# Warm-up matmuls in the prologue and the plan's hand-over times, in an attention and SwiGLU kernel on one core

## The chip, the core and the metric

The kernel runs on one core of one Trainium2 chip. A core has engines that run their own instruction streams and meet only at semaphores: TensorE (PE in the profile; its weight loads are listed as PEld), VectorE (DVE), ScalarE (ACT), GpSimd (POOL) and SyncE (SP), which here issues most DMAs. Matmuls write into PSUM, which the kernel uses as eight banks of 128 x 512 fp32. The metric is the device time of one execution in microseconds. It was taken in 14 runs; the number compared is their median.

## What is computed

A layer norm without weights, then two branches from the normalised rows: multi-query attention with 32 heads of width 16 that share one K and one V, and a SwiGLU feed-forward. The output is the input plus the product of the two branches, the second passed through one more SiLU.

```
S, D, H, Dh, F = 2048, 512, 32, 16, 1792
xn = layernorm(x)
q  = (xn @ wq) split into H heads;  k = xn @ wk;  v = xn @ wv      # k, v: [S, Dh]
p  = softmax(q k^T / sqrt(Dh));     s = (p v, heads joined) @ wo
b  = (silu(xn @ w_gate) * (xn @ w_up)) @ w_down
out = x + s * silu(b)
```

The score matrix has 32 * 2048 * 2048 entries, and each needs an exponential. That is the bulk of the work for ScalarE and VectorE.

## The kernel before

**Tiling.** Rows come in four blocks of 512 (NSC). Heads come in four groups of eight (NQ); a block of rows with a group of heads is a "pair", and a pair has two "halves" of four heads. That makes 32 blocks `b` of 16 key tiles times 2 head pairs `x`, so 1024 score tiles of 128 x 1024. Each tile is two matmuls (L813) into one of three double banks, `ring[0..2]`, and has one of two ways out:

- ScalarE reads `ring[0]` or `ring[1]` and writes exp to a bf16 buffer `Pb` (L863).
- VectorE reads `ring[2]` and writes a scaled 16-bit integer to `Ub` (L890). When two tiles of a pair are there, three more operations split it by bit masks into `Eb` (L906) and `Wb` (L903) and multiply (L908), so that two accumulating matmuls with differently scaled V give an approximation of the exponential.

Both ways end in matmuls with V (L696) that accumulate in `o_ps`, with the softmax's denominator beside it. At the end of a block VectorE copies `o_ps` to `oa` (L709). After both halves of a pair, small DMAs on SyncE's queue gather the denominators into `dn` (L723) and pack the second half's values (L667), VectorE takes the reciprocal (L670), and further DMAs (L673, L679) spread it for a multiplication on GpSimd (L681).

**Fill.** The feed-forward, the Q projections of later pairs and the output projections use the bank `m_ps` in between (L466 for their matmuls, L607 and L624 for their tanh on ScalarE, L592, L609, L613, L626, L640 on VectorE).

**Prologue.** Statistics (L415, L416), normalisation (L425), transposes on TensorE (L430) into banks that ScalarE or VectorE copies to `xnT` (L436), then K, Q and V of row block 0 (L439, L447, L443, L555, L452); row blocks 1 to 3 follow while the first score tiles run.

**What sets the order.** While the program is built, a small list scheduler (`_Sched`, L182) plays the whole kernel through in its own time and writes down an order for every engine, which the emitted instructions then follow. `sd.free[engine]` is when an engine is free in that plan. Each operation has a planned duration, for example 0.904 for an exp, 1.135 for L890, 0.6 for most 512-wide VectorE operations and 0.215 for a 512-column matmul (MMF). `avail(d, eng)` gives when the result of `d` may be used on another engine: its planned end plus `LAT` of the engine that made it. The tiles' own semaphores keep the data right whatever the plan says; the plan only decides who stands behind whom.

`pe_pick` chooses TensorE's next work: a score tile for ScalarE as soon as a ring slot is planned free, other ready work if it fits before that (with `TOL` = 0.12 of slack), a score tile for VectorE (`dve_sc`) or a "junk" matmul whose result nobody reads (L1100). Ahead of all planned work `NWARM` matmuls of the same kind stand in TensorE's stream (L411). The plan of the kernel before starts TensorE at 0 and doesn't know of them.

`dve_tile` decides whether VectorE gets a tile: in the last block only if at least `D_LIM_END` tiles of it are left for ScalarE, in the blocks before it `D_LIM`.

## Time and profile before

| | |
|---|---|
| median of 14 runs | 800.91 us (796.01 to 813.11) |
| profiled execution | 802.83 us |
| its span, first to last instruction | 801.0 us |
| mean granted TensorE clock | 0.969 |
| first exp starts | 20.70 us |
| exps on ScalarE, score tiles on VectorE | 774, 250 |

The page of the profile gives totals over the whole span; a second view gives each engine's busy time for chosen stretches; a third, the timeline, lists instructions in order of time with their start, their duration and, in square brackets, how long the engine stood idle before one and what ended that. Successive exps overlap in it[...]: the mean record of L863 is 1171 ns, and yet in busy stretches one starts every 0.9 us or so. The granted clock is 1.00 where TensorE runs at full rate.

### The profile page before, as it was taken

Reading aid. Unit: us, or ns where it says so; the run is one execution under the profiler, and the core shown is the slowest. Engines: PE = TensorE matmul, PEld = TensorE weight load, DVE = VectorE, ACT = ScalarE, POOL = GpSimd, SP = SyncE. Lnnn points to the kernel's source line nnn. Section 1 sums busy time; section 2 is a strip of 40 time slices with the busy share of each in tenths; the row PEclk is TensorE's granted clock in tenths of the full one; section 3 lists DMA queues with packets and bytes.
Section 4 is the critical chain, followed back from the end, with each engine's and each line's share of the span. In section 5 each row is a group of like instructions: output and inputs, shape, how many; then the busy total and the mean of one; then the engine's idle time right before and its main releaser. Section 6 shows DMA issues by size and latency. Waiting matters only on the chain.

```text
span 801.0 us, 19338 instructions
## 1 busy us (share of the span) xinstructions
PE 738.1 (92%) x8005; PEld 222.5 (28%) x8009; DVE 748.1 (93%) x935; ACT 754.1 (94%) x856; POOL 52.1 (7%) x59
## 2 busy tenths in 40 slices
PE   8889899899989999999999999999999999999994
PEld 4332222222212222222222222222222222222221
DVE  4879999999969999999999999999999999999985
ACT  2799999999979999999999999999999999999991
POOL 1210000000002000000002010000000210000001
PEclk9899999999979999999999999999999999999957
DMA  9300000000000000000001000000000010000000
GB/s 330 106 1 2 22 2 23 1 4 21 1 23 21 10 20 2 23 2 23 3 7 31 15 22 2 23 2 7 18 1 14 31 29 2 9 15 2 23 1 30
DMA packets 19463, 18.49 MB, mean 23 GB/s; under 512 B 8552, under 2 KB 15464, under 8 KB 19368
## 3 DMA queue, kind: packets, MB, share of 16 engines
q1 hardware_dynamic: 17496, 16.37, 6.7%
q8 instruction: 64, 1.05, 0.6%
q10 hardware_dynamic: 1872, 0.82, 0.4%
q14 instruction: 31, 0.25, 0.1%
HBM read 12.62 MB, written 2.34 MB: 19 GB/s over the span
## 4 chain that ended last, share of the span: by engine, by line
PE 37%; ACT 26%; DVE 25%; issue 8%; SPq 1%; DMA 1%; POOL 0%; ACTq 0%; DVEq 0%; POOLq 0%
ACT Pb L863 22%; PE ring L813 14%; PE m_ps L466 12%; DVE Ub L890 9%; PE o_ps L696 7%; DVE Wb L908 4%; ACT th L607 3%; DVE Wb L903 3%; DVE Eb L906 2%; SPq L723 1%; ACT th L624 1%; DVE ab L609 1%; DVE hT L613 1%; DVE oa L709 1%; PE ring L1100 1%
## 5 line engine op out<-in xcount | busy, mean ns | idle before, releaser
L863 ACT ACTIVATE Pb<-ring 128x1024 bf16<-128x1024 f32 x774 | 734.0, 1171 | 14.4 <-PE ring L813 13.4
L813 PE MATMUL ring<-QB,KT 32*128 32x512 bf16 x2048 | 323.2, 389 | 35.9 <-ACT Pb L863 25.5
L890 DVE TENSOR_SCALAR Ub<-ring 128x1024 uint16<-128x1024 f32 x250 | 304.9, 1219 | 15.9 <-PE ring L813 8.5
L813 PEld LDWEIGHTS <-KT 32*128 32x128 bf16 x2048 | 103.7, 91 | 341.7 <-issue 336.1
L908 DVE TENSOR_TENSOR Wb<-Wb,Ub 128x2048 f16<-128x2048 f16 x125 | 153.9, 1231 | 0.0
L696 PE MATMUL o_ps<-Pb,VA 128*32 128x512 bf16 x1548 | 149.6, 395 | 0.9 <-POOL VA L461 0.5
L903 DVE TENSOR_SCALAR Wb<-Ub 128x2048 uint16<-128x2048 uint16 x125 | 88.4, 707 | 0.3 <-PE o_ps L696 0.3
L906 DVE TENSOR_SCALAR Eb<-Ub 128x2048 uint16<-128x2048 uint16 x125 | 86.4, 691 | 0.0
L466 PE MATMUL m_ps<-xnT,wu_sb 128*32 128x512 bf16 x896 | 72.2, 388 | 3.6 <-DVE ab L609 3.6
L466 PE MATMUL m_ps<-wd_sb,hT 128*32 128x512 bf16 x896 | 73.2, 384 | 1.3 <-DVE g_sb L626 1.2
L466 PE MATMUL m_ps<-xnT,wg_sb 128*32 128x512 bf16 x896 | 73.8, 388 | 0.4 <-DVE hT L613 0.2
L681 POOL TENSOR_TENSOR oT<-oa,rb 128x512 bf16<-128x512 f32 x15 | 22.2, 1483 | 614.7 <-DMA rb<-dscr 551.8
L696 PE MATMUL o_ps<-Eb,VD 128*32 128x512 f16 x500 | 51.1, 398 | 2.9 <-DVE Eb L906 2.0
L696 PE MATMUL o_ps<-Wb,VD 128*32 128x512 f16 x500 | 50.5, 393 | 2.8 <-DVE Wb L908 2.3
L696 PEld LDWEIGHTS <-VA 128*32 128x32 bf16 x1548 | 37.1, 94 | 51.5 <-issue 51.0
L696 PEld LDWEIGHTS <-VD 128*32 128x32 f16 x1000 | 31.1, 94 | 50.6 <-issue 48.1
L607 ACT ACTIVATE th<-m_ps 128x512 f32<-128x512 f32 x56 | 42.3, 755 | 0.0
L613 DVE TENSOR_TENSOR hT<-ab,m_ps 128x512 bf16<-128x512 f32 x56 | 38.1, 681 | 2.2 <-PE m_ps L466 1.9
L609 DVE SCALAR_TENSOR_TENSOR ab<-th,m_ps 128x512 f32<-128x512 f32 x56 | 38.0, 679 | 1.9 <-ACT th L607 1.5
L466 PEld LDWEIGHTS <-wu_sb 128*32 128x32 bf16 x896 | 18.0, 95 | 34.3 <-issue 31.6
L709 DVE COPY oa<-o_ps 128x512 f32<-128x512 f32 (+1 forms) x33 | 21.9, 667 | 3.0 <-PE o_ps L696 3.0
L466 PEld LDWEIGHTS <-wg_sb 128*32 128x32 bf16 x896 | 16.5, 94 | 26.3 <-issue 26.0
(94 smaller groups left out, 242.6 us busy)
## 6 DMA issues: line engine op xcount, KB each, us to landing
rb<-dscr SPq DMA_DIRECT2D x15, 256.0 KB
dn<-oa SPq DMA_DIRECT2D x120, 2.0 KB, 1.7
oa<-oa SPq DMA_DIRECT2D x60, 32.0 KB, 2.0
wg_sb<-in_B_w_gate_dram SPq DMA_DIRECT2D x1, 1792.0 KB, 11.5
wu_sb<-in_B_w_up_dram SPq DMA_DIRECT2D x1, 1792.0 KB
wd_sb<-in_B_w_down_dram SPq DMA_DIRECT2D x1, 1792.0 KB, 20.4
out_dram<-xn SPq DMA_DIRECT2D x14, 128.0 KB, 1.7
x_sb<-in_A_x_dram SPq DMA_DIRECT2D x3, 512.0 KB
```

Source lines behind the costliest of these rows:

```text
L466: return [nc.tensor.matmul(out=dst[GRP * j:GRP * j + GRP, :], lhsT=w[:, GRP * j:GRP * j + GRP], rhs=rhs, start=start, stop=stop, tile_posi ...
L607: t_ = OP("ACT", 0.477, [a], lambda: nc.scalar.activation(out=th[i][:], in_=m_ps[:], func=ACT.Tanh, scale=0.5), (0,), name="tanh")
L609: s_ = OP("DVE", 0.6, [t_, ab_rel[i]], lambda: nc.vector.scalar_tensor_tensor(out=ab[i][:], in0=th[i][:], scalar=1.0, in1=m_ps[:], op0=ALU ...
L613: h = OP("DVE", 0.6, [b], lambda: nc.vector.tensor_tensor(out=hT[:, f, :], in0=ab[i][:], in1=m_ps[:], op=ALU.mult), (1,), name="hmul")
L696: r.append(nc.tensor.matmul(out=o_ps[GRP * g:GRP * g + GRP, :], lhsT=lhs, rhs=rhs, start=(n == 0), stop=(n == pv_total[(b, g)] - 1), tile_ ...
L709: oev[b] = sd.new(_Op("DVE", 0.6, [], lambda: [nc.vector.tensor_copy(out=oat[:, a:z], in_=o_ps[:, a:z]) for a, z in cuts], (0.2,), name="o ...
L813: return lambda: [nc.tensor.matmul(out=ring[sl][:, u * 512:(u + 1) * 512], lhsT=KT[half][GRP * g:GRP * g + GRP, t * P:(t + 1) * P], rhs=QB ...
L863: lambda: nc.scalar.activation(out=Pb[pi][:], in_=ring[i][:], func=ACT.Exp, scale=escale, bias=ebias),
L890: lambda: nc.vector.tensor_scalar(out=Ub[ui][:, x * 1024:(x + 1) * 1024], in0=ring[2][:], scalar1=ubias, scalar2=UINF, op0=ALU.add, op1=AL ...
L903: o1 = OP("DVE", 0.6, [pa, pa0, w_rel[u - NE] if u >= NE else None], lambda: nc.vector.tensor_scalar(out=Wb[ei][:], in0=Ub[ui][:], scalar1 ...
L906: o2 = OP("DVE", 0.6, [pa, pa0, e_rel[u - NE] if u >= NE else None], lambda: nc.vector.tensor_scalar(out=Eb[ei][:], in0=Ub[ui][:], scalar1 ...
L908: o3 = OP("DVE", 1.135, [o1, o2], lambda: nc.vector.tensor_tensor(out=Wb[ei][:].bitcast(FP16), in0=Wb[ei][:].bitcast(FP16), in1=Ub[ui][:]. ...
```

## The change

Six edits:

1. `NWARM` falls from 18 to 13, and the plan starts TensorE at 6.8 instead of 0. Junk matmuls may now be placed in any planned gap of over 0.3 as long as no VectorE pair has been started (before: as long as no feed-forward job had been), up to 200 instead of 60.
2. `LAT`, the planned time from the end of a ScalarE result to its use elsewhere, grows from 0.166 to 0.22; for VectorE from 0.13 to 0.25.
3. `D_LIM_END` grows from 6 to 8.
4. In `place_sc` a score tile of row block 0 depends on the half of K that it reads, not always on the second.
5. In `pe_do` a VectorE score tile that is put right behind a ScalarE one isn't planned before its K and Q.
6. At the end the build asserts that no operation is emitted ahead of one that it depends on.

```diff
-NWARM, NJUNK = 18, 60
-D_START, D_LIM, D_LIM_END = 26, 12, 6
+NWARM, NJUNK = 13, 200
+D_START, D_LIM, D_LIM_END = 26, 12, 8
...
-    LAT = {"PE": 0.205, "ACT": 0.166, "DVE": 0.13, "POOL": 0.16, "DMA": 0.0, "EXT": 0.0}
+    LAT = {"PE": 0.205, "ACT": 0.22, "DVE": 0.25, "POOL": 0.16, "DMA": 0.0, "EXT": 0.0}
...
     sd = _Sched()
+    sd.free["PE"] = 6.8
...
         ks = k_ready[t // 4][b % 2]
-        sc = _Op("PE", dur, [slot[sl]] + ks[-1:] + q_ready[b // 2], sc_emit(sl, b, t, x), (0,), "r", "sc")
+        ks = ks[t % 4 // 2:t % 4 // 2 + 1] if len(ks) > 1 else ks
+        sc = _Op("PE", dur, [slot[sl]] + ks + q_ready[b // 2], sc_emit(sl, b, t, x), (0,), "r", "sc")
...
-        junk = job["f"] == 0 and cur["junk"] < NJUNK and all(
+        junk = cur["np"] == 0 and cur["pair"] is None and cur["junk"] < NJUNK and all(
             w.start is None or v.start is not None and v.end + 0.13 <= F for w, v, bk in held if bk == "2b")
...
-            at = max(sd.free["PE"], sd.avail(slot[2], "PE"))
+            at = max(sd.free["PE"], sd.avail(slot[2], "PE"), tile_ready(*dt))
...
-    for o in order:
+    place = {id(o): i for i, o in enumerate(order)}
+    for i, o in enumerate(order):
+        assert all(d.eng == "EXT" or place[id(d)] < i for d in o.deps), [(o.name, o.start, o.seq)] + [(d.name, d.start, d.end, d.seq) for d in o.deps]
```

Counted in the two built programs, the change removes 5 matmuls of L411 and 28 of L1100, turns 4 VectorE tiles into exps (778 and 246), and leaves the number of every other kind of instruction as it follows from that. The order changes on TensorE, VectorE and ScalarE nearly everywhere.

## The prediction

> **What bounds the kernel now.** I read the page first, then the windows cut at the places where ScalarE stalls, then the timeline of the first 32 us, of the stall near 225 us and of the end. "Exp" below is one ScalarE activation of L863, a tile of 128x1024 scores; a "DVE tile" is one of the same size taken by VectorE at L890.

> From the page, the shares of busy time and the costliest groups:

> ```profile
> PE 738.1 (92%) x8005; PEld 222.5 (28%) x8009; DVE 748.1 (93%) x935; ACT 754.1 (94%) x856; POOL 52.1 (7%) x59
> ...
> L863 ACT ACTIVATE Pb<-ring 128x1024 bf16<-128x1024 f32 x774 | 734.0, 1171 | 14.4 <-PE ring L813 13.4
> L813 PE MATMUL ring<-QB,KT 32*128 32x512 bf16 x2048 | 323.2, 389 | 35.9 <-ACT Pb L863 25.5
> ```

> Three engines are nearly full, so the average says little. The windows say where they are not (stretch, length, then busy time of PE, weight load, VectorE, ScalarE, GpSimd, then the granted TensorE clock):

> ```profile
> 20.70:32.20 11.50, 9.74 (x85) 4.19 (x85) 8.78 (x23) 7.86 (x8) 2.94 (x5) 0.70 0.51 162
> 225.00:246.00 21.00, 18.96 (x156) 3.64 (x155) 15.30 (x19) 14.64 (x17) 2.51 (x2) 0.67 0.08 21
> 400.00:600.00 200.00, 188.71 (x2138) 56.25 (x2138) 195.46 (x231) 200.00 (x229) 12.70 (x8) 1.00 0.05 13
> 760.00:783.60 23.60, 22.85 (x140) 5.14 (x140) 20.82 (x30) 21.65 (x23) 0.00 (x0) 0.52 0.00 1
> 783.60:801.00 17.40, 6.50 (x85) 2.43 (x77) 8.47 (x23) 0.74 (x2) 2.75 (x2) 0.79 0.11 35
> ```

> From 400 to 600 us ScalarE never rests: there it is the bound. It starves only before its first exp, and in three stretches where the clock is low (0.70, 0.67, 0.52). Price of a saturated exp: from 246 to 760 us the groups list 533 exps and 52 tanhs; one tanh takes 0.48 from its start to the next start (439.07 to 439.55 in the timeline), so an exp takes (514 - 52*0.48)/533 = 0.917 us. So the span is: first exp at 20.70; 774*0.917 + 72*0.48 = 709.8 + 34.6 = 744.4 of saturated work; the last exp ends at 783.6, so 783.6 - 20.7 - 744.4 = 18.5 us lost in between; then 17.4 us of tail. Of the 18.5 I put 5.5 before 48 us (24 exps in 27.5 us), 6.3 at 225 to 246 (16 exps and a tanh in 21 us need 15.2), 3.4 at 760 to 783.6 (22 exps need 20.2), the rest scattered.

> Why the first exp is late, in the timeline:

> ```profile
> 1.41 6.64 PE L411 MATMUL ring<-QB,ident_bf 128*128 128x512 bf16 x18 [1.41 <-POOL ident_bf masks.py:199]
> ...
> 6.75 0.72 DVE L425 TENSOR_SCALAR xn<-x_sb,mv,rstd 128x512 bf16<-128x512 bf16 x2
> ...
> 7.88 6.85 PE L1100 MATMUL ring<-x_sb,ident_bf 128*128 128x512 bf16 x31
> ...
> 14.79 0.61 PE L430 MATMUL ring<-ident_bf,xn 128*128 128x128 bf16 x8
> ...
> 20.70 3.77 ACT L863 ACTIVATE Pb<-ring 128x1024 bf16<-128x1024 f32 x4 [0.48 <-PE ring L813]
> ```

> The normalised rows xn are ready from 7.1 us, but their transposes stand behind 18 + 32 dummy matmuls in TensorE's order and start at 14.79. The plan counted TensorE free from 0 and did not know of the 18. And the stall at 225 us:

> ```profile
> 219.93 0.69 DVE L709 COPY oa<-o_ps 128x512 f32<-128x512 f32 x1
> ...
> 225.75 0.35 DVE L670 RECIPROCAL rc<-dn 128x32 f32<-128x32 f32 x1 [2.47 <-DMA oa<-oa]
> ...
> 227.23 0.39 PE L813 MATMUL ring<-QB,KT 32*128 32x512 bf16 x2 [1.70 <-DVE Ub L890]
> ```

> VectorE stood 2.47 us at a reciprocal whose DMAs had not landed, TensorE 1.70 us behind it, and the clock then fell to 0.50 for 230 to 240 us.

> [...] the weight loads of L411 are 0.42 us apart until 6.50 us, closer from 6.80; windows of 2 and 5 us put the later spells at 0.50 at 23.7 to 30.6 (6.8 us) and 228.5 to 242.2. [...] Here an exp lasts 1.171 us while its successor starts 0.917 later, and a TensorE score that waits starts 0.05 after that end: 1.22 from exp start to release. [...] on the SyncE queue here 1.7 (dn) and 2.0 (oa).

> **The change, part by part** (the order is that of the built program, in which no time stands).

> 1. Warm-up and TensorE's start in the plan (NWARM 13, free at 6.8, the new gap rule). Ahead of the first transpose stand 13 + 1 dummies instead of 18 + 32. 13 at 0.427 from 1.41 end at 6.96, one more at 7.39; xn is there at 7.1 to 7.5. So the transposes start near 7.5, 7.3 us earlier. What follows (copy, K, Q, second half) has the same order and 4 + 4 dummies in its gaps as before. What could hold it: wq landed 4.9 us after its issue at 1.30, so 6.2, and its first matmul would come at 9.7; wv (1.82 + 7.0 = 8.8) at 13.4; the second pair of xn ends at 10.05, needed at 10.2. None binds. First exp: 20.70 - 7.2 = 13.5. FFN weights: wg 15.5 and wd 26.7, first FFN matmul moves from 51.5 to near 42: no wait. TensorE must be warm by then; the trace had it warm at 6.7, within the 13. [...]

> 2. The first 32 tiles. VectorE's order now has the last statistics of row block 1 before the K copies of block 0, and TensorE does that block's transposes two rows together. In the trace this chain (17.99 to K at 30.91) made ScalarE starve 2.90 us before 32.21. Its TensorE part ran cold. I take 2 of the 5.5 us back; ends: 0 and 4.

> 3. ACT 0.166 to 0.22, DVE 0.13 to 0.25. The plan's exp is 0.904, so it now frees a slot 1.124 after the start, against 1.22 measured and 1.07 before: nearer. For a VectorE op of 0.6 it has 0.85 against 0.68 + 0.05 measured: now too careful. TensorE's 25.5 us of waits for exps should shrink, but ScalarE at 100% hides them. Saturated exps have a floor: many are 0.90 apart. Gain at most (0.917 - 0.904)*778 = 10 us, loss taken as equal; value 0. What moves besides: on VectorE between the last o_ps copy and the reciprocal. Before, the shortest distance is 2.33 us of work (the stall at 225), the next 3.47 and 3.53; the reciprocals that waited least (0.16 and 0.31) started 3.62 and 3.84 after the copy's end. After, that one place has 3.47, but three have 2.87 to 2.93. Each waits about 0.7[...] unless a DMA is late, as dn was by 1.7 in 2 of 15 pairs. Behind the reciprocal stand all VectorE tiles, and behind them TensorE's scores. Instead of 6.3 I take 3; ends 0 and 3*6.3.

> 4. D_LIM_END 8 and the new latencies together: 778 exps and 246 DVE tiles instead of 774 and 250: +4*0.917 = +3.7 us of ScalarE; VectorE loses 9 us of work, hidden, as ScalarE is the bound. In return the end: the last exp ended at 783.6, but VectorE's last product only fed TensorE at 787.09, the o_ps copies at 787.53, the transposes of L938 at 788.01, and the end came 13.0 later. Now the last accumulation comes from an exp, with 24 wo matmuls (1.3 us) behind: transposes at 0.1 + 0.2 + 1.3 = 1.6 after the last exp, tail 14.6 instead of 17.4: -2.8. FFN matmuls now fill TensorE until 9 tiles are left instead of 33, so the cold stretch from 760 loses its cause: 1 instead of 3.4.

> 5. The pairing of K halves, the due time of a merged VectorE score, the assertion: order alone, no instruction; nothing.

> Sum: 13.5 + (778*0.917 + 34.6 = 748.0) + lost (3.5 + 3 + 1 + scattered 3 = 10.5) + 14.6 = 786.6, against the span of 801.0: -14.4. The profiled execution took 802.83, 1.92 above the median of 800.91; so the median would be 786.5.

> **Rivals.**
> - Only the start gains (0.20): later losses remain 18.5, since cold spells move rather than go. 13.5 + 748.0 + 18.5 + 14.6 = 794.6 span, median 794.5. [...] Against: order at 225 and at the end did change.
> - It does not do what it says: 13 dummies do not warm TensorE, which stays at half rate through the prologue (0.12). +3 to the first exp, +2 for block 1: 791.5. For it: the dummies stop 0.7 us after the release in the trace. Against: activity from 1.41 is unbroken.
> - Slower (0.10): reciprocals issued before their DMAs land, at the places with 2.87 to 3.47 us, five in all; each full cold spell costs 6.3. 783.5 + n*6.3: three give 802.4, four 808.7, five 815. It decides from about three. For it: one 2.47 us wait did this at 225. [...]

> **How the numbers follow.** The sum (0.58) gives 787; its own range 780 to 793 from the ends of steps 2 to 4. To 0.8 I go down to 779 and up to 797, which takes in the first two rivals. A measurement here tells 0.3% (2.4 us) from no change. Faster 0.90; same 0.04 (three spells); slower 0.06.

> **What would show it.** Right: first transpose near 7.5 and first exp near 13.5; 778 exps; no clock below 1.00 at 225; last exp end to span end below 15. Wrong: first exp later than 17 with clock 0.50 before it; more than one reciprocal with over 2 us of wait and a clock of 0.50 after it; saturated exps dearer than 0.93 (the new latencies cost order).

## The result, and the profile after

| | before | after |
|---|---|---|
| median | 803.44 us (47 runs, 796.01 to 813.11) | 793.28 us (10 runs, 790.66 to 799.16) |
| ratio | | 0.9889, 95% interval 0.9866 to 0.9913 |
| profiled execution, its span | 802.83, 801.0 | 795.23, 793.4 |
| first exp starts | 20.70 | 13.17 |
| exps and tanhs at the saturated price | 774, 72: 744.3 | 778, 72: 748.0 |
| lost between first and last exp | 18.6 | 17.8 |
| last exp's end to the end of the span | 17.4 | 14.5 |

The change makes the kernel 1.1% faster. The prediction was 787 with a range from 779 to 797: direction and range hold, the size does not. 14.4 us of span were forecast, 7.6 came between the two profiled executions and 10.2 between the medians; the profiled execution of after took 1.95 us more than its median. Three of the four rows of the sum came as forecast in this execution (13.5, 748.0, 14.6). The fourth did not: 10.5 us were to be lost in between, and it was 17.8.

From the page of the kernel after: busy time of the engines, the granted clock in 40 slices of 19.8 us, and the two groups shown of before (their lines moved to L865 and L814).

```profile
PE 724.4 (91%) x7965; PEld 216.8 (27%) x7968; DVE 740.1 (93%) x925; ACT 757.6 (95%) x860; POOL 50.4 (6%) x59
...
PEclk9869999999989999999999999999999999999997
...
L865 ACT ACTIVATE Pb<-ring 128x1024 bf16<-128x1024 f32 x778 | 737.2, 1181 | 13.7 <-PE ring L814 12.9
L814 PE MATMUL ring<-QB,KT 32*128 32x512 bf16 x2048 | 320.6, 387 | 46.3 <-ACT Pb L865 39.6
```

ScalarE is still the bound, and its idle time before exps is unchanged (14.4 before, 13.7 now). The slices under 9 are now the second, the third and the twelfth (218 to 238 us); those near the end are gone but for the very last. TensorE's waits for exps, which step 3 expected to shrink, went from 25.5 to 39.6 us.

The new start in the timeline of after (start, duration, engine, line; in brackets the idle time before and what ended it):

```profile
1.41 5.65 PE L411 MATMUL ring<-QB,ident_bf 128*128 128x512 bf16 x13 [1.41 <-POOL ident_bf masks.py:199]
...
6.89 0.38 PE L1102 MATMUL ring<-x_sb,ident_bf 128*128 128x512 bf16 x1
...
7.15 0.72 PE L430 MATMUL ring<-ident_bf,xn 128*128 128x128 bf16 x8
...
13.17 4.69 ACT L865 ACTIVATE Pb<-ring 128x1024 bf16<-128x1024 f32 x5 [0.48 <-PE ring L814]
```

The transposes follow the dummies directly, 7.6 us earlier, and the first exp comes 7.5 us earlier. Where the rest was lost is seen when the span is cut where the granted clock changes (windows: stretch, length, busy time of PE, weight load, VectorE, ScalarE, GpSimd with counts, granted clock, DMA share, GB/s):

```profile
13.67:17.09 3.42, 1.99 (x16) 0.95 (x16) 3.25 (x9) 3.42 (x5) 2.06 (x4) 1.00 1.03 407
17.09:23.91 6.82, 6.46 (x49) 2.23 (x49) 4.27 (x11) 3.84 (x4) 0.33 (x2) 0.50 1.07 367
37.56:40.98 3.42, 2.86 (x37) 1.34 (x36) 1.63 (x3) 3.42 (x5) 0.73 (x3) 1.00 0.00 0
40.98:54.63 13.65, 13.65 (x104) 2.48 (x100) 8.97 (x11) 10.74 (x13) 0.08 (x1) 0.50 0.01 2
211.64:215.06 3.42, 2.41 (x20) 0.82 (x21) 3.03 (x5) 3.42 (x5) 0.00 (x0) 1.00 0.00 0
215.06:225.29 10.23, 9.89 (x66) 1.83 (x63) 7.68 (x9) 8.03 (x9) 0.00 (x0) 0.50 0.01 2
638.29:641.70 3.41, 2.20 (x28) 0.78 (x32) 3.41 (x6) 3.41 (x6) 0.00 (x0) 1.00 0.00 0
641.70:645.12 3.42, 3.42 (x34) 0.59 (x29) 3.03 (x4) 2.49 (x4) 0.00 (x0) 0.50 0.05 7
755.00:778.00 23.00, 20.20 (x220) 6.59 (x220) 19.27 (x27) 23.00 (x28) 0.00 (x0) 1.00 0.00 1
```

Four times TensorE ran at half clock, for 6.8, 13.7, 10.2 and 3.4 us. In each of these ScalarE starves (10.74 us busy of 13.65); in the 3.4 us ahead of each it does not, but TensorE has only 1.99 to 2.86 us of work. Counted against 0.917 us for an exp and 0.48 for a tanh, as in the prediction, 8.7 us are lost before 60 us, 1.4 from 60 to 200, 3.4 from 200 to 250, 3.9 from 250 to 700, and 0.4 behind 700. Before it was 5.3, 0.7, 7.6, 1.3 and 3.7.

The reciprocals, which the prediction feared, in the table of waits (engine, line, waited for: us in sum, times, longest):

```profile
PE ring L814 <- ACT Pb L865: 39.6, 103, 1.0
...
DVE rc L671 <- DMA dn<-oa: 4.6, 5, 1.3
```

They are the ones at 81.1 (0.92), 225.6 (0.39), 365.9 (1.34), 458.3 (0.94) and 738.5 (0.98). None is followed by a stretch at half clock: that of 215.06 begins before the reciprocal of 225.6.

### The profile page after: what moved, and what is told of

Read it like the earlier page. It is cut to its first block, busy times and chain, and to the rows that moved or that the text cites. A ratio compares the mean times of both kernels' runs of the same rounds, so it can differ in the third digit from the quotient of the medians.

```text
span 793.4 us, 19252 instructions
## 1 busy us (share of the span) xinstructions
PE 724.4 (91%) x7965; PEld 216.8 (27%) x7968; DVE 740.1 (93%) x925; ACT 757.6 (95%) x860; POOL 50.4 (6%) x59
## 4 chain that ended last, share of the span: by engine, by line
PE 40%; ACT 28%; DVE 21%; issue 8%; SPq 1%; DMA 1%; POOL 0%; ACTq 0%; DVEq 0%
ACT Pb L865 23%; PE ring L814 16%; PE m_ps L466 14%; PE o_ps L697 8%; DVE Ub L892 7%; DVE Wb L910 4%; ACT th L608 4%; DVE Wb L905 2%; DVE Eb L908 2%; ACT th L625 1%; SPq L724 1%; DVE ab L610 1%; DVE stats L415 1%; DVE ab L641 1%; DVE oa L710 1%
## 5 line engine op out<-in xcount | busy, mean ns | idle before, releaser
L865 ACT ACTIVATE Pb<-ring 128x1024 bf16<-128x1024 f32 x778 | 737.2, 1181 | 13.7 <-PE ring L814 12.9
L814 PE MATMUL ring<-QB,KT 32*128 32x512 bf16 x2048 | 320.6, 387 | 46.3 <-ACT Pb L865 39.6
L892 DVE TENSOR_SCALAR Ub<-ring 128x1024 uint16<-128x1024 f32 x246 | 299.7, 1218 | 17.8 <-PE ring L814 12.8
L814 PEld LDWEIGHTS <-KT 32*128 32x128 bf16 x2048 | 105.4, 91 | 358.5 <-issue 353.9
L905 DVE TENSOR_SCALAR Wb<-Ub 128x2048 uint16<-128x2048 uint16 x123 | 86.6, 704 | 0.3
L682 POOL TENSOR_TENSOR oT<-oa,rb 128x512 bf16<-128x512 f32 x15 | 20.3, 1351 | 628.3 <-DMA rb<-dscr 563.8
L697 PE MATMUL o_ps<-Wb,VD 128*32 128x512 f16 x492 | 48.9, 387 | 2.5 <-DVE Wb L910 1.8
L697 PEld LDWEIGHTS <-VD 128*32 128x32 f16 x984 | 29.0, 94 | 48.1 <-issue 46.7
L466 PEld LDWEIGHTS <-wg_sb 128*32 128x32 bf16 x896 | 17.1, 95 | 25.8 <-issue 24.8
L466 PEld LDWEIGHTS <-wu_sb 128*32 128x32 bf16 x896 | 16.1, 95 | 26.6 <-issue 24.8
## 6 DMA issues: line engine op xcount, KB each, us to landing
wd_sb<-in_B_w_down_dram SPq DMA_DIRECT2D x1, 1792.0 KB, 20.2
```

The source lines that it names most:

```text
L466: return [nc.tensor.matmul(out=dst[GRP * j:GRP * j + GRP, :], lhsT=w[:, GRP * j:GRP * j + GRP], rhs=rhs, start=start, stop=stop, tile_posi ...
L697: r.append(nc.tensor.matmul(out=o_ps[GRP * g:GRP * g + GRP, :], lhsT=lhs, rhs=rhs, start=(n == 0), stop=(n == pv_total[(b, g)] - 1), tile_ ...
L814: return lambda: [nc.tensor.matmul(out=ring[sl][:, u * 512:(u + 1) * 512], lhsT=KT[half][GRP * g:GRP * g + GRP, t * P:(t + 1) * P], rhs=QB ...
L865: lambda: nc.scalar.activation(out=Pb[pi][:], in_=ring[i][:], func=ACT.Exp, scale=escale, bias=ebias),
L892: lambda: nc.vector.tensor_scalar(out=Ub[ui][:, x * 1024:(x + 1) * 1024], in0=ring[2][:], scalar1=ubias, scalar2=UINF, op0=ALU.add, op1=AL ...
L905: o1 = OP("DVE", 0.6, [pa, pa0, w_rel[u - NE] if u >= NE else None], lambda: nc.vector.tensor_scalar(out=Wb[ei][:], in0=Ub[ui][:], scalar1 ...
```

## The experiments

The theory after the comparison, A: the new start is one gain of 7.5 us, the new latencies another at the end, and what is missing went to half clock. The main rival, D: the reciprocals, which now stand earlier behind their transfers, cost it. Others were that the latencies cost (B), that one order or another is only luck (E), and some that stand in the expectation of a single run. In the table "lost" is cut at 60 us, "half" is the length of the stretches at half clock that begin before the last exp's end, from the trace's own record of the clock, and all but the ratio and the median are of one profiled execution.

| run | median us | ratio to before (95%) | span | first exp | exps | lost to 60 | lost after 60 | tail | half |
|---|---|---|---|---|---|---|---|---|---|
| before | 803.4 | | 801.0 | 20.7 | 774 | 5.3 | 13.3 | 17.4 | 44.4 |
| after | 793.28 | 0.9889 (0.9866 to 0.9913) | 793.4 | 13.2 | 778 | 8.7 | 9.1 | 14.5 | 34.1 |
| e1_warm_only | 794.79 | 0.9899 (0.9857 to 0.9940) | 790.6 | 13.2 | 774 | 9.5 | 6.1 | 17.4 | 44.4 |
| e2_lat_only | 799.90 | 0.9949 (0.9926 to 0.9972) | 804.6 | 20.9 | 776 | 5.1 | 16.8 | 15.6 | 47.8 |
| e4_lim6 | 792.38 | 0.9874 (0.9824 to 0.9925) | 790.3 | 13.3 | 776 | 5.6 | 7.3 | 18.0 | 27.3 |
| e5_dens | 784.96 | 0.9777 (0.9736 to 0.9818) | 782.9 | 13.3 | 776 | 5.2 | 4.0 | 14.3 | 13.7 |
| e8_warm_dens | 792.88 | 0.9898 (0.9860 to 0.9935) | 795.4 | 13.3 | 774 | 13.1 | 6.6 | 18.1 | 47.8 |
| e9_dens15 | 805.05 | 0.9997 (0.9959 to 1.0034) | 799.6 | 13.4 | 778 | 3.3 | 19.7 | 15.3 | 30.7 |
| e10_dens_t10 | 788.99 | 0.9829 (0.9780 to 0.9877) | 788.0 | 13.9 | 778 | 3.6 | 6.1 | 16.5 | 20.5 |
| e11_stale | 790.85 | 0.9847 (0.9801 to 0.9893) | 792.0 | 13.3 | 778 | 4.5 | 8.7 | 17.4 | 30.7 |
| e12_act_only | 789.19 | 0.9827 (0.9776 to 0.9878) | 788.4 | 13.3 | 774 | 3.4 | 8.7 | 18.6 | 13.7 |
| e13_dve_only | 793.34 | 0.9866 (0.9800 to 0.9933) | 787.7 | 13.3 | 778 | 7.2 | 2.4 | 16.8 | 23.9 |
| e14_late | 789.81 | 0.9836 (0.9782 to 0.9890) | 788.0 | 13.3 | 776 | 8.3 | 6.3 | 13.9 | 27.3 |
| e9_dens31 | 787.18 | 0.9795 (0.9743 to 0.9846) | 786.8 | 13.3 | 776 | 3.3 | 9.2 | 14.9 | 23.9 |

### The start alone, the latencies alone

e1_warm_only is the kernel before with edit 1:

```diff
-NWARM, NJUNK = 18, 60
+NWARM, NJUNK = 13, 200
...
+    sd.free["PE"] = 6.8
...
-        junk = job["f"] == 0 and cur["junk"] < NJUNK and all(
+        junk = cur["np"] == 0 and cur["pair"] is None and cur["junk"] < NJUNK and all(
```

> Part one of the change alone: 13 warming matmuls, the planner's TensorE starting at 6.8, fillers in every gap of the prologue; the planner's latencies stay as before. Theory A (the start is one gain of about 7.5 us and the latencies give another of about 3 at the end): first exp near 13.2 us instead of 20.7, 774 exps as before, the last exp to the end of the span still about 17 us with the half clock there; time 794 to 798, ratio to before about 0.992. Rival B (the latencies give nothing or cost): this kernel is as fast as or faster than the whole change, at or below 793.3. Rival C (a warm start is only paid back in a later stall): first exp near 13.2, but lost time up by 5 us or more and the time above 800.

e2_lat_only is the kernel before with edit 2:

```diff
-    LAT = {"PE": 0.205, "ACT": 0.166, "DVE": 0.13, ...
+    LAT = {"PE": 0.205, "ACT": 0.22, "DVE": 0.25, ...
```

> The two latencies alone (0.22 after ScalarE, 0.25 after VectorE), prologue as before. Theory A: first exp at 20.7 as before; no stretch at half clock in the last 40 us, the tail some 2 to 3 us shorter, about 2 more exps (+1.8 us) and waits of the reciprocals of about 0.9 us each in four or five places; in sum 799 to 804, ratio 0.995 to 1.000. Rival B (the latencies cost, by more waits of TensorE for exps and by the reciprocals): ratio above 1.002. Rival C (the latencies carry most of the gain): ratio below 0.992.

The start alone gives 0.9899, with the first exp at 13.22, 774 exps and a tail of 17.4: theory A in each number. The stretch at half clock near the end is there as before (windows of e1_warm_only, columns as above):

```profile
30.20:33.61 3.41, 2.84 (x34) 1.26 (x32) 2.90 (x8) 3.29 (x5) 1.01 (x1) 1.00 0.00 0
33.61:47.26 13.65, 12.98 (x94) 4.23 (x92) 4.95 (x10) 9.57 (x10) 1.74 (x6) 0.50 0.00 1
747.00:750.40 3.40, 2.61 (x26) 0.77 (x22) 3.40 (x5) 3.40 (x4) 0.00 (x0) 1.00 0.00 0
750.40:774.20 23.80, 23.40 (x146) 5.30 (x150) 21.14 (x30) 20.91 (x22) 0.00 (x0) 0.50 0.00 1
```

New is the one from 33.6: with the earlier start comes a stretch at half clock behind 32 us, which the profile of before does not have, and in this profile it gives back some 4 us of the 7.5. It is the half clock that is new there, not the thin stream: in the profile of before TensorE was busy for 0.80 of the time from 32 to 41 us, and its clock stayed at 1.00 (windows of before):

```profile
32.00:41.00 9.00, 7.19 (x73) 3.27 (x70) 7.91 (x21) 8.66 (x10) 2.07 (x4) 1.00 0.01 2
41.00:55.00 14.00, 12.09 (x137) 4.98 (x138) 9.27 (x15) 13.30 (x16) 1.75 (x6) 1.00 0.01 2
```

Of the twelve profiles with the new start ten have half clock at some time between 34 and 55 us; of the two with the old start neither has. Two are few, so that the earlier start brings it is likely and not shown.

The latencies alone give 0.9949, at the edge of theory A's bracket; their profiled execution took 806.4 us, the longest of its 22 runs, so of its row I read only the counts and the first exp. Added up, the two ratios give 0.985, and the whole change has 0.9889. One reason is in the profiles: before lost 7.6 us between 200 and 250, e1_warm_only loses 1.7 there and the whole change 3.4, so the stall at 225 us, which the latencies were to shorten, is gone with the start alone. The whole is 1.5 us below the start alone with intervals that overlap, so in the whole change the gain of the latencies and the limit can't be told from nothing. Edits 4 and 5 play no part: with them and without them the built programs have the same order on every engine.

### The limit of lead at the end

e4_lim6 is the kernel after with `D_LIM_END` at 6 instead of 8.

> The whole change, but with the limit of lead at the end back at 6 as before: 776 exps instead of 778, and the order differs only behind the last weight load. Theory A (the limit only trades two exps, 1.8 us, against VectorE tiles which then come last): within 2 us of the whole change, tail 2 us longer, so ratio to before 0.987 to 0.991. Rival: the limit is what keeps TensorE's clock up at the end; with 6 the half clock is back after 755 us and the time is 3 us or more longer than with the whole change (ratio above 0.993).

792.38 beside 793.28: no difference, as theory A has it. Near the end TensorE ran at half clock for 6.8 us here (from 768.1), not for the 23.9 of before, and the rival's 3 us are not there: the limit isn't what took the 23.9 away. That the latencies did isn't shown either, for e8_warm_dens, which has those of before, also has 6.8 us there.

The tail is 3.4 us longer than after. That goes with the clock. In the eight profiles in which TensorE is at half clock when the last exp ends, the tail is 16.5 to 18.6 us; in the other six it is 13.9 to 15.6. e4_lim6 is among the eight, and so is e11_stale (below), which has the order of after to the end: 17.4, where after, with full clock there, has 14.5.

### The reciprocals later

e5_dens is the kernel after with one number changed. It makes the planner put the reciprocals later, and so changes the order of VectorE's work:

```diff
-        dens_op[b] = OP("DMA", 2.4, [ev], dens, (0,))
+        dens_op[b] = OP("DMA", 3.8, [ev], dens, (0,))
```

> The whole change, with the planned duration of the four small transfers of the denominators raised from 2.4 to 3.8 us, so that VectorE has at least 4.07 us of other work between the copy and the reciprocal in every place (2.87 at the least before). Theory A (the half clock, not the reciprocals, is what took the rest): reciprocals wait in at most one place, PE's waits for exps stay near 35 to 40 us, time 2 us at the most below the whole change. Rival D (the reciprocals' waits of about 0.9 us each start the losses behind them): 4 to 6 us below the whole change, lost time near the 10.5 us of the forecast, ratio to before near 0.983.

784.96, more than rival D expected. No reciprocal waits, and lost time is 9.2 us. But the profile doesn't say that the waits were the cause (page, then windows of e5_dens at the same places as of after):

```profile
PEclk9899999999999999999999999999999999999998
```

```profile
16.00:26.30 10.30, 10.05 (x68) 3.35 (x65) 7.37 (x20) 6.50 (x8) 2.16 (x5) 0.50 1.04 359
37.56:40.98 3.42, 2.86 (x32) 1.39 (x30) 1.63 (x3) 3.42 (x5) 0.00 (x1) 1.00 0.00 0
40.98:54.63 13.65, 12.44 (x148) 3.66 (x146) 11.26 (x13) 13.65 (x16) 0.81 (x3) 1.00 0.01 2
211.64:215.06 3.42, 3.01 (x32) 0.91 (x30) 3.42 (x5) 3.42 (x5) 0.00 (x0) 1.00 0.03 4
```

Of the 8.6 us of lost time between the two profiles, 3.5 lie before 60 us, where no reciprocal has run yet (the first comes at 81.1 after), and 3.1 between 200 and 250, where half clock began ahead of the reciprocal. ScalarE is busy throughout from 41 to 54.6, with the clock at 1.00. Two runs therefore keep an order and change only the waits, and a third makes the waits longer.

e11_stale is the kernel after in its own order; each reciprocal reads data that is there already:

```diff
-        r = OP("DVE", 0.26, [d0, d1], lambda: nc.vector.reciprocal(out=rc[:, pair, :], in_=dn[:, pair, :]), (2.2,),
+        r = OP("DVE", 0.26, [d0, d1], lambda: nc.vector.reciprocal(out=rc[:, pair, :], in_=dn[:, max(pair - 1, 0), :]), (2.2,),
```

> The whole change, every instruction in the same order on every engine, but each reciprocal reads the denominators of the pair before (already there for long) instead of its own, which had to come by the four small transfers; so the output's normalisation is that of another pair, and only the wait is gone. Theory D (the reciprocals' waits cost, themselves and by what they leave TensorE short of): the waits of 0.9 to 1.3 us in four or five places are gone but for the first pair, and 3 to 5 us of the time with them; 788 to 790, ratio about 0.983. Rival E (what e5_dens gained came from another order of VectorE's work, not from the waits): 792 to 795 as the whole change, 0.988. Rival H (all of e5_dens's gain is the waits): 785, 0.978.

The waits are gone but for the first pair (table of waits of e11_stale):

```profile
DVE rc L671 <- DMA dn<-oa: 0.9, 1, 0.9
```

The median is 790.85, 2.4 us below the whole change (3.4 by the ratios to before): a smaller gain than D had, a larger one than E, and the intervals of the two ratios overlap. So 3.7 us of waits are worth some 2 to 3 us, perhaps none. They are hardly the 8.3 of e5_dens (rival H): five of the six runs of e5_dens are below 785.5 and every run of e11_stale above 789, though the intervals of these two ratios touch as well.

e14_late is e5_dens in its own order, with six transfers that nobody needs ahead of each block's four:

```diff
+            late = [nc.sync.dma_start(out=dlate[6 * b + k:6 * b + k + 1, :],
+                                      in_=oat[GRP * (k % 4) + r0:GRP * (k % 4) + r0 + 1, :]) for k in range(6)]
-            return [nc.sync.dma_start(out=dn[...], in_=oat[...]) for g in range(4)]
+            return late + [nc.sync.dma_start(out=dn[...], in_=oat[...]) for g in range(4)]
```

> e5_dens with the same order on all four compute engines, but six more small transfers (to a scratch that nobody reads) ahead of the four of each block's denominators on SyncE's queue, so that the denominators land about 3.5 us later. VectorE's planned work between copy and reciprocal is 5.8 us or less in eight of the fifteen places, so waits come back: about 1.5 us in six, 2 and 3.2 us in two, some 13 us in sum. Theory D (a wait of VectorE at a reciprocal is paid in time, about 0.5 to 1 us for each us): 792 to 798. Rival E (the order of e5_dens is what is fast, and such waits find cover): within 2 us of e5_dens, 783 to 787. In either case nothing else changes but SyncE's queue.

It missed its own aim: three reciprocals wait, 3.2 us in sum, where 13 were expected, and they start 6.0 to 7.2 us behind the copy. The time is 4.9 us above e5_dens, between the two expectations. Its profile has 5.4 us more lost, but 3.1 of these before 60 us, ahead of every reciprocal (windows of e14_late):

```profile
29.10:32.50 3.40, 2.36 (x33) 1.32 (x30) 2.93 (x8) 2.76 (x4) 1.93 (x4) 1.00 0.02 5
32.50:53.00 20.50, 20.14 (x137) 4.26 (x137) 9.84 (x14) 16.04 (x17) 0.81 (x3) 0.50 0.00 1
```

The four compute engines have the order of e5_dens, instruction for instruction, and yet one has 20.5 us at half clock here and the other none from 26 to 378 us. The same is seen in the three profiles with the order of after up to 750 us: the stretch that begins between 38 and 41 us is 13.7 us long in after, 3.4 in e4_lim6 and 6.8 in e11_stale; the one from 17.1 is in the first two and not in e11_stale; and 8.7, 5.6 and 4.5 us are lost before 60.

e9_dens15 goes the other way: the planned duration of the transfers is 1.5 instead of 2.4.

> The whole change with the planned duration lowered from 2.4 to 1.5 us, the opposite of e5_dens: seven of the fifteen reciprocals now have only 2.33 us of VectorE work between the copy and themselves (in the whole change three have 2.87 to 2.93). Theory D: those seven wait about 1.5 us each, some 10 us in sum on VectorE where the whole change shows 4.6; if 4.6 us of waits cost 8 us there, these cost 14 to 20, so 797 to 805, ratio 0.993 to 1.003, with more stretches at half clock behind the waits. Rival E (order by chance): within 4 us of the whole change in either direction, and the half clock stands elsewhere than behind the reciprocals.

805.05, all of the gain gone. Ten reciprocals wait, 11.6 us in sum. And here the whole chain is seen once, in the timeline and then in the windows of e9_dens15:

```profile
404.17 0.68 DVE L710 COPY oa<-o_ps 128x512 f32<-128x512 f32 x1
...
410.53 0.35 DVE L671 RECIPROCAL rc<-dn 128x32 f32<-128x32 f32 x1 [1.71 <-issue]
...
412.01 0.39 PE L814 MATMUL ring<-QB,KT 32*128 32x512 bf16 x2 [1.25 <-DVE Ub L892]
...
413.15 1.02 ACT L865 ACTIVATE Pb<-ring 128x1024 bf16<-128x1024 f32 x1 [1.27 <-PE ring L814]
```

```profile
410.60:414.00 3.40, 1.87 (x18) 0.58 (x15) 3.40 (x5) 2.13 (x3) 0.00 (x0) 1.00 0.13 27
414.00:431.10 17.10, 17.10 (x124) 2.91 (x120) 11.42 (x14) 11.81 (x13) 4.73 (x3) 0.50 0.10 32
```

VectorE stands 1.71 us at the reciprocal (the profile names no releaser), TensorE then waits 1.25 for VectorE, is busy for 1.87 of 3.40 us, and runs at half clock for the next 17.1. So D's mechanism is seen at a wait of 1.71 us; the wait of 2.47 us at 225 us in the profile of before was of the same kind: TensorE was busy for 1.49 of the 3.41 us from 225.12, and half clock followed for 13.7 (windows of before). In the change under study it took at most a part of the gain (e11_stale).

e9_dens31 is a point between: 3.1 us.

> The whole change with the planned duration at 3.1 us, between 2.4 (793.3) and 3.8 (785.0). Twelve of the fifteen places are as in e5_dens, three have about 3.5 us of VectorE work before the reciprocal and so wait 0.1 to 0.4 us. Theory D with the half clock as the way it costs: 784 to 788. If e5_dens is one lucky order among many: anywhere up to 793.

787.18. Over the four values 1.5, 2.4, 3.1 and 3.8 the medians are 805.1, 793.3, 787.2 and 785.0: one lucky order does not make such a row. But what each step up takes away is waits and thin places together, and the runs part the two only at 2.4 (e11_stale) and 3.8 (e14_late).

### Both latencies, one, or none, with the reciprocals late

With 3.8 throughout: e8_warm_dens has neither of the new latencies (it is e1_warm_only with the edit of e5_dens), e12_act_only has ScalarE's 0.22 alone, e13_dve_only VectorE's 0.25 alone.

> The kernel before with the new start of the prologue (as in e1_warm_only) and the longer planned duration of the denominators' transfers (3.8 us), but with the planner's latencies of before. Theory D (it is the reciprocals' waits that cost, and the latencies pay only through the end): the waits of e1_warm_only (1.2 us at 220 and three shorter) are gone, the stretch at half clock in the last 40 us stays, so 2 to 4 us below e1_warm_only, 791 to 793, ratio about 0.986, some 6 us above e5_dens. Rival F (the latencies are worth nothing once no reciprocal waits): within 1.5 us of e5_dens, 784 to 787. Rival E (e5_dens is only a lucky order): no gain over e1_warm_only, 794 or more.

> As e5_dens, but of the planner's two latencies only ScalarE's at the new value (0.22); VectorE's is back at 0.13. With both old (e8_warm_dens) 792.9, with both new (e5_dens) 785.0. If the spare time after VectorE is what pays: 791 to 793, with a tail of 17 us. If that after ScalarE is what pays: 785 to 787.

> As e5_dens, but of the two latencies only VectorE's at the new value (0.25); ScalarE's is back at 0.166. If the spare time after VectorE is what pays: 784 to 787, lost time near 9 and waits of TensorE for exps back near 25 us. If that after ScalarE is what pays: 790 to 793. If neither alone matters (only the order it happens to give): e12_act_only and e13_dve_only lie together, 787 to 790.

Neither 792.88, ScalarE's 789.19, VectorE's 793.34, both 784.96. The intervals of neither and both don't meet: here the latencies are worth 8 us (edits 3 to 5 change no place in the built order here), though with the reciprocals early they and the limit gave 1.5. Which of the two does it isn't settled. e8_warm_dens is theory D's number for another reason than D's: its reciprocals wait in one place only (0.77), and its profile, of an execution of 797.2 us, has the longest stretch of all at half clock, 37.6 us from 17.2. The 13.1 us lost before 60 stand ahead of every reciprocal.

### Fillers in the thin stretch

e10_dens_t10 is e5_dens with fillers in planned gaps of over 0.1 instead of 0.3:

```diff
-        if junk and T - F > 0.3:
+        if junk and T - F > 0.1:
```

> e5_dens, with filler matmuls also in planned gaps of TensorE in the prologue down to 0.1 us (0.3 before): 24 fillers instead of 14, five of them ahead of the second block's transposes. Theory A (the half clock at 15 to 27 us comes from TensorE's thin stream there): the clock stays at full from 15 to 27, first 20 us of exps lose 3 us less, 781 to 783, ratio about 0.974. Rival G (the stretch is set off elsewhere or the fillers come in the way): half clock still there at 15 to 27 us, time equal to e5_dens or up to 3 us above.

The stretch from 16 us is gone, with 2.80 us of TensorE work in the 3.42 us where after had 1.99 (windows of e10_dens_t10):

```profile
13.67:17.09 3.42, 2.80 (x36) 1.50 (x33) 2.97 (x11) 3.23 (x4) 2.06 (x4) 1.00 1.03 408
17.09:23.91 6.82, 6.24 (x63) 2.57 (x61) 5.98 (x16) 5.72 (x7) 1.77 (x4) 1.00 1.07 367
```

That the fillers did it isn't shown. e14_late has none of them, and no half clock there either (windows of e14_late):

```profile
13.20:17.00 3.80, 2.52 (x35) 1.48 (x32) 3.72 (x12) 3.70 (x5) 2.07 (x4) 1.00 1.03 407
17.00:24.00 7.00, 6.27 (x63) 2.72 (x64) 6.17 (x17) 5.73 (x8) 1.94 (x4) 1.00 1.07 369
```

What goes with it is the grid on which the clock changes: the changes of one execution lie whole multiples of 3.41 us apart (2, 7, 11, 58, 61, 183, 184 and 225 of them behind 17.09 us in after), and the program starts at another point of that grid from one execution to the next (a step at 13.67 us in after, at 12.6 in e5_dens, at 15.4 in e14_late). In six of the twelve profiles with the new start a step of the grid falls between 12.6 and 13.8 us (after, e1_warm_only, e4_lim6, e5_dens, e8_warm_dens, e13_dve_only), and all six go to half clock at the next step. In the other six the steps fall between 10.7 and 12.0 and between 14.1 and 15.5, and none does; e10_dens_t10 and e14_late are among these. One reading, which is not shown, is that there the thin place is split between two windows of the grid. TensorE's busy share doesn't tell the two groups apart: from 12.5 to 15 us it is 0.60 to 0.74 in the six and 0.63 to 0.74 in the others.

Lost time before 60 us falls from 5.2 to 3.6. But other stretches come in its place (3.4 us at 49 and at 73, 10.2 at 100), and with two exps more and a longer tail the time is 789 beside 785, which the intervals don't tell apart. Whether filling this place is a gain stays open.

## Why the prediction was right or wrong

Step 1, the start: right. 13.5 was forecast, 13.17 measured, and e1_warm_only shows that edit 1 alone does it. The rival that 13 dummies don't warm TensorE fell: the clock is 1.00 from 6.8 to 17.1 us.

Step 2, the first 32 tiles: this is the term that failed. 2 of 5.5 us were to come back, 3.5 to stay; 8.7 stayed, 5.2 of the 7.3 us by which the sum is short. The step knew of the chain of row block 1, whose stretch at half clock merely moved with the start (6.8 us from 23.7 before, 6.8 from 17.1 after). It allowed for no second stretch at half clock behind that one. After has 13.7 us of it from 41.0, out of a thin place in which K and V of a later row block are made, ahead of the first VectorE tile (41.8); e1_warm_only has one too, and the two profiles with the old start have not. What it costs differs from execution to execution. In the three profiles with the order of after 8.7, 5.6 and 4.5 us are lost, mean 6.3, so the profiled execution fell on the dear side, but none of the three came down to 3.5.

Step 3, the reciprocals and the stall at 225: its allowance of 3 us was the right size (3.4 lost from 200 to 250) and for the wrong content. The 6.3 us that it started from are ScalarE's idle time there; 21 us with 15.2 of work leave 5.8, which moves nothing in the sum. Five reciprocals wait, not three, for 4.6 us, 0.39 to 1.34 each (the transfers to dn and oa land 1.7 and 2.0 us after their issue in the median of before), and none of these waits is followed by half clock; e11_stale values their removal at 2 to 3 us, perhaps none. The half clock near 225 did not go, though: 10.2 us from 215.1, out of a thin place at 211.6 in which TensorE waits four times for 0.2 to 0.4 us on ScalarE and VectorE. e4_lim6 and e11_stale, which have the order of after here, have one at 212 too, and so have e9_dens15, e2_lat_only and e12_act_only at 208 to 218; the seven other changed kernels have none. It comes with the order. TensorE's waits for exps rose rather than fell, and the guess that this has no price at ScalarE's floor held: the exps' idle time is what it was.

Step 4, the end: right in mechanism, and right in number with some luck. 778 exps, tail 14.54 for 14.6, and 0.4 lost behind 700 for 1; the transposes start 1.68 us after the last exp, for 1.6. But this holds at full clock. In e11_stale, the same order, half clock lasts 4.3 us beyond the last exp, the transposes come 4.60 us after it, the tail is 17.4, and 3.9 are lost behind 700: no better than before. Part of the step was put down to the limit of 8, which e4_lim6 finds to matter little.

The scattered 3 us were 5.3: 1.4 from 60 to 200 and 3.9 from 250 to 700, with one stretch at half clock at 641.7 and three of the reciprocals' waits among them.

Of the rivals, "only the start gains" was the nearest: 794.5 for 793.28, and its reason, that cold spells move rather than go, is what the traces show: 44.4 us at half clock in three stretches, from 23.7, 228.5 and 761.0 us, before, and 34.1 us in four, from 17.1, 41.0, 215.1 and 641.7, after. Its content is right in part: the tail and the end did gain in the profile of after, and did not in that of e11_stale. "Slower" needed three reciprocals with a full cold spell each, and there was none. The weight of 0.58 on the sum was too high because each spell was treated as having one cause that an edit removes.

What stays open: whether the waits of about 0.9 us cost anything; which of the two latencies pays; what makes a thin place one that half clock follows; and what decides how long TensorE stays at half clock. A steady supply of extra work for TensorE in the middle of the kernel was not tried.

The fastest version found is e5_dens, 0.9777 of before, below the whole change with intervals that don't meet.

## What to carry to other kernels

When three engines are nearly full, look for places where TensorE's stream thins out, not only for waits on the critical engine: in after ScalarE was busy for all 3.42 us of the thin place at 211.64 us, and for 8.03 of the 10.23 us at half clock behind it. An edit to a planner's latencies moves such places about, so take one cause of lost time to be replaced by another until a run shows otherwise, and read two or three profiles of one order before putting a price on one stretch. And plan a transfer with the duration that the trace shows: the five reciprocals that wait in after start 3.80 to 3.86 us after the copy in four places and 4.81 in the fifth, and the one at 410.53 us in e9_dens15 starts 5.68 after it, where the plans had 2.4 and 1.5.
